# A spectral layer and expert routing on one Trainium2 core: the length-2048 transform split as 64 by 32 in place of 128 by 16, with quarter-array products and a new issue order

## The chip, the core and the metric

The kernel runs on one core of a Trainium2 chip. The core has five engines with queues of their own: TensorE (PE, matrix products; its weight loads are shown as PEld), VectorE (DVE), ScalarE (ACT), GpSimd (POOL) and SyncE (SP, which here only issues the DMAs). They meet through semaphores. Data lies in SBUF (128 partitions), and products land in PSUM, which has eight banks of 2 KB per partition. The metric is the device time of one execution in microseconds; lower is better.

## What is computed

`x` has 2048 rows of 576 numbers. It is normalised by rows to `xn`; the result is `x + A(xn) + B(xn)`.

```python
def _A_ref(x, w_r, w_i):                      # a filter in the spectrum
    X = rfft2(x)                              # over 2048 rows and 576 columns
    return irfft2(X * (w_r + 1j * w_i))

def _B_ref(x, w_q, k1, k2, u, v):             # 32 heads, 8 by 8 experts, the best one per head
    q = einsum("nd,dhc->nhc", xf, w_q)
    s1 = einsum("nhd,ed->nhe", q[..., :128], k1)
    s2 = einsum("nhd,ed->nhe", q[..., 128:], k2)
    e = argmax(s1) * 8 + argmax(s2)           # K = 1, so the softmax weight is 1
    return einsum("nh,nhd->nd", gelu(einsum("nd,nhd->nh", xf, u[e])), v[e])
```

## The kernel before

**The spectral branch.** The length-2048 transform is split as 128 by 16: row `16 n + t` is point `n` of slice `t`. `ln`, `folds` and `dft128` normalise, fold the 576 columns to even and odd halves and do the 128-point step, one slice `t` at a time, as f32 products with the matrix `Rs`. The result is kept as two f16 parts (high and remainder) in `AB` and `ABL`. Then there are 16 groups `g` of frequencies. For each, `d_fwd` does the 576-point step (14 f16 products), after which ACT copies the result from PSUM to f16 and DVE subtracts to get the f16 remainder; `s_fwd` does the 16-point step with the twiddle factors for two groups at once, as 48 f16 products of 64 by 64 on quarters of the PE array (high by high, remainder by high, high by remainder); `s_mul` multiplies by the filter; `s_inv` and `d_inv` go back, and `fin` does the inverse 128-point step for one slice `t` as two f32 products of the whole array (one for each half of the 576 columns).

**The routing branch.** `fold_part` multiplies the keys into `w_q` (18.9 MB, 32 loads named `w<-in_wq`) on quarter strips of the array, 32 columns wide. For each of eight row blocks `r`, `x_t` loads and splits the transposed `x`; `scores` makes the scores relative to expert 0 for 64 lists of seven (28 products of 512 columns), their maximum `mx`, and a mask `eq` of where the maximum is; `route` turns the masks into codes, powers of two that say which expert won, and multiplies and adds them to one matrix of weights; `combine` splits these into f16 high and remainder parts, and PE transposes them (two per block) into `CAT`. `fin` adds `CAT` times the table `vS` (four f16 products of the whole array for each `t`), adds `x`, and stores the slice.

**The order of the work.** Each call on an engine is recorded as an operation of a planner (`_Plan`); neighbouring products are joined to one operation of up to about 0.9 us by the planner's own costs. `forward` then lists all operations: each engine, whenever free, takes the ready one with the lowest number in the table `RANK` (1295 entries, one per operation, in the order of the program text). The resulting order is fixed in the instruction streams, each engine runs its own in order, and SP's stream of DMAs likewise. A DMA into a buffer that is used again waits for the buffer, and what stands behind it on SP waits too. All instructions are issued by one helper, so that they all have line 527 in the profile; they are told apart by tile names. There `A` stands for the buffers of `F`, `A2` and `yy` together, `t` for `t1`, `t2` and the folds, `MT` for the routing's small tables and `CAT`, `w` for the routing's masks and the loads of `w_q`.

Of the kernel before, what the change touches and what calls it, by code (L numbers as in the profile page):

```python
# [10 lines left out]
F32 = mybir.dt.float32  # L11
F16 = mybir.dt.float16
# [20 lines left out]
def _consts():  # L33
    pi2 = 2 * np.pi
    n1 = np.arange(128)
    R = np.zeros((128, 16, 4, 2))
    for k in range(64):
        g, a = divmod(k, 4)
        if k == 0:
            R[:, g, a, 0] = 1.0  # L40
            R[:, g, a, 1] = (-1.0) ** n1
        else:
            R[:, g, a, 0] = np.cos(pi2 * (k * n1 % 128) / 128)
            R[:, g, a, 1] = -np.sin(pi2 * (k * n1 % 128) / 128)
    R = _clean(R.reshape(128, 128))
    c32 = np.stack([R * 2.0 ** -7, R.T * 0.5, np.eye(128)], 1).astype(np.float32)

    U = np.zeros((16, 16, 4, 2, 16, 2, 4))
    V = np.zeros_like(U)
    n2 = np.arange(16)[:, None]  # L50
    k2 = np.arange(16)[None, :]
    kk = np.zeros((16, 16, 2, 4), int)
    for g in range(16):
        for a in range(4):
            k1 = 4 * g + a
            if k1 == 0:
                for s in range(2):
                    ph = pi2 * ((64 * s + 128 * k2) * n2 % 2048) / 2048
                    U[g, :, a, s, :, s, a] = np.cos(ph)
                    V[g, :, a, s, :, s, a] = -np.sin(ph)  # L60
                    kk[g, :, s, a] = 64 * s + 128 * np.arange(16)
            else:
                ph = pi2 * ((k1 + 128 * k2) * n2 % 2048) / 2048
                for s, sg in ((0, 1), (1, -1)):
                    U[g, :, a, 0, :, s, a] = np.cos(ph)
                    U[g, :, a, 1, :, s, a] = np.sin(ph)
                    V[g, :, a, 0, :, s, a] = -sg * np.sin(ph)
                    V[g, :, a, 1, :, s, a] = sg * np.cos(ph)
                    kk[g, :, s, a] = (sg * (k1 + 128 * np.arange(16))) % 2048
    U = _clean(U.reshape(16, 128, 128))  # L70
    V = _clean(V.reshape(16, 128, 128))


    pair = np.arange(128).reshape(16, 2, 2, 2).transpose(2, 0, 1, 3).ravel()
    row = np.arange(128).reshape(16, 2, 2, 2).transpose(1, 0, 2, 3).ravel()
    kk = kk.reshape(16, 128)[:, pair]
    U, V = U[:, :, pair], V[:, :, pair]

    def halves(m):
        return np.concatenate([m[:, :64, :64], m[:, 64:, 64:]], 1)  # L80

    def tr(m):
        m = m.transpose(0, 2, 1).reshape(16, 128, 16, 8).transpose(0, 1, 3, 2).reshape(16, 128, 128)
        return halves(m)

    Ut, Vt = tr(U), tr(V)
    iv = np.concatenate([Ut, Vt, -Ut], 2)
    U, V = halves(U[:, row]), halves(V[:, row])
# [3 lines left out]
    s16 = np.concatenate(_hl(fw * 64) + _hl(iv), 2)  # L92
# [446 lines left out]
def _body(ctx, tc, nc, plan, a, out):  # L539
# [413 lines left out]
    def combine(r):  # L953
# [15 lines left out]
        for i in range(2):  # L969
            P.transpose(pc[:, i, :], chl[:, i, :], id16)  # L970
# [263 lines left out]
```

## Time and profile before

| | |
|---|---|
| median of 3 runs | 223.67 us (222.45 to 223.74) |
| span of the profiled execution, first to last instruction | 220.8 us |
| PE busy in the span | 196.7 us |
| DVE busy | 193.2 us |
| POOL busy | 146.0 us |
| ACT busy | 136.8 us |
| read from and written to memory | 38.33 MB, 4.72 MB |

The profiled execution has no time of its own beside its span; the span is 2.87 us below the median of the timed runs, which also hold what lies ahead of the first and behind the last instruction. A product in f32 appears as two records in the profile (so `x64` of the f32 products in `fin` are 32 products). The ends of products are modelled, so consecutive starts, not the durations, tell what one costs in a stream.

### The profile page before, as it was taken

What the parts mean: (1) busy time and instruction counts of PE and PEld (TensorE: products, weight loads), DVE (VectorE), ACT (ScalarE), POOL (GpSimd) and SP (SyncE); (2) the same over time, 40 slices, a digit from 0 to 9 for tenths busy, and PEclk for the clock granted to TensorE, in tenths of its full rate; (3) what the DMA queues carried; (4) which work ended last, traced back from release to release, by engine and by line L of the source; (5) the groups of instructions that cost most, each with busy time, mean ns of one, the idle gap of its engine ahead of it and who ended that gap; (6) DMA issues with size and microseconds to landing.
All of it is one profiled execution on the core that took longest, in us unless ns stands there. A gap on an engine that the chain in (4) does not pass through costs nothing.

```text
span 220.8 us, 5961 instructions
## 1 busy us (share of the span) xinstructions
PE 196.7 (89%) x2287; PEld 134.9 (61%) x2287; DVE 193.2 (88%) x423; ACT 136.8 (62%) x297; POOL 146.0 (66%) x201
## 2 busy tenths in 40 slices
PE   0079789999999999899998999899999899999993
PEld 0048367766866658466565666455566577788872
DVE  1886999998599879639999998999999999999973
ACT  2096987986499788986769658585652323332330
POOL 3987887960209962854598349687946656686890
PEclk9999999999999999999999999999999999999999
DMA  6999999999999991634246310410000012123225
GB/s 205 405 425 416 408 410 405 389 354 353 367 410 411 406 370 64 202 98 109 96 123 196 118 56 11 148 39 4 1 3 0 0 56 107 53 109 125 91 113 210
DMA packets 14572, 43.43 MB, mean 197 GB/s; under 512 B 1872, under 2 KB 4688, under 8 KB 14160
## 3 DMA queue, kind: packets, MB, share of 16 engines
q1 hardware_dynamic: 14544, 43.05, 52.5%
q8 instruction: 18, 0.29, 0.5%
q14 instruction: 10, 0.08, 0.1%
HBM read 38.33 MB, written 4.72 MB: 195 GB/s over the span
## 4 chain that ended last, share of the span: by engine, by line
PE 48%; DVE 23%; ACT 13%; issue 6%; DMA 5%; POOL 3%; SPq 0%; DVEq 0%; POOLq 0%; ACTq 0%
PE banks L527 48%; DVE t L527 5%; DMA xf<-in_xT_dram 4%; DVE w L527 4%; DVE MT L527 3%; DVE A L527 3%; ACT t L527 2%; ACT xf L527 2%; DVE mx L527 2%; DVE AB L527 2%; DMA kT<-in_kT_dram 2%; ACT AB L527 1%; POOL yh L527 1%; DVE st L527 1%; ACT A L527 1%
## 5 line engine op out<-in xcount | busy, mean ns | idle before, releaser
L527 PE MATMUL banks<-MU,xT 128*128 128x512 f16 x192 | 47.9, 379 | 1.0 <-ACT A L527 0.6
L527 POOL TENSOR_TENSOR xT<-xf,xT 128x640 f16<-128x640 f32 x16 | 23.2, 1455 | 19.5 <-ACT xf L527 19.5
L527 PE MATMUL banks<-c,AB 128*128 128x145 f16 (+1 forms) x384 | 34.6, 227 | 0.0
L527 PEld LDWEIGHTS <-xT 128*128 128x128 f16 x224 | 20.6, 99 | 21.9 <-issue 1.3
L527 PEld LDWEIGHTS <-AB 128*128 128x128 f16 x384 | 31.7, 122 | 3.4 <-issue 1.6
L527 POOL TENSOR_TENSOR A<-t 128x145 f32<-128x145 f32 (+2 forms) x48 | 30.3, 647 | 4.0 <-DVE t L527 1.5
L527 POOL TENSOR_TENSOR y<-t,t 128x289 f32<-128x289 f32 x32 | 21.6, 697 | 14.7 <-DVE t L527 14.5
L527 POOL TENSOR_TENSOR yh<-y,yh 128x578 f16<-128x578 f32 x16 | 23.4, 1470 | 6.8 <-issue 3.0
L527 POOL TENSOR_TENSOR t<-XN 128x289 f32<-128x289 f32 x32 | 24.9, 799 | 4.3 <-DVE A L527 3.0
L527 DVE SCALAR_TENSOR_TENSOR t<-banks,wx,Wt 128x578 f32<-128x578 f32 x32 | 24.3, 808 | 0.3 <-PE banks L527 0.3
L527 DVE TENSOR_TENSOR AB<-banks,AB 128x512 f16<-128x512 f32 x32 | 21.6, 679 | 1.9 <-ACT AB L527 1.1
L527 PE MATMUL banks<-w,KP 128*32 128x288 f32 x256 | 21.5, 432 | 1.8 <-DMA w<-in_wq_dram 1.5
L527 ACT ACTIVATE yh<-banks,sc 128x580 f32<-128x580 f32 x16 | 11.7, 744 | 17.6 <-PE banks L527 13.6
L527 PE MATMUL banks<-Rs,yl 128*99 128x128 f32 x64 | 10.9, 302 | 13.1 <-ACT Rs L527 13.1
L527 ACT ACTIVATE AB<-banks 128x512 f16<-128x512 f32 x32 | 18.8, 590 | 4.6 <-PE banks L527 4.5
L527 PE MATMUL banks<-A,c 128*128 128x288 f32 x64 | 21.4, 416 | 0.0
L527 PE MATMUL banks<-c,ABL 99*128 99x289 f16 (+1 forms) x64 | 18.5, 289 | 2.3 <-DVE AB L527 0.9
L527 PEld LDWEIGHTS banks<-Rs,A 128*128 128x128 f32 x128 | 16.3, 202 | 3.7 <-DVE A L527 1.8
L527 DVE TENSOR_TENSOR ABL<-banks,ABL 33x256 f16<-33x256 f32 x32 | 12.9, 407 | 6.4 <-ACT AB L527 5.3
L527 PEld LDWEIGHTS banks<-Rs,yl 128*99 128x99 f32 x64 | 8.3, 180 | 16.6 <-ACT Rs L527 15.7
L527 PE MATMUL banks<-Rs,A 128*128 128x128 f32 x128 | 18.2, 292 | 0.0
L527 DVE TENSOR_REDUCE MT<-w 128x128 bf16<-128x896 bf16 (+1 forms) x16 | 18.1, 1143 | 0.1
(124 smaller groups left out, 433.5 us busy)
## 6 DMA issues: line engine op xcount, KB each, us to landing
w<-in_wq_dram SPq DMA_DIRECT2D x32, 576.0 KB, 7.6
xf<-in_xT_dram SPq DMA_DIRECT2D x16, 320.0 KB, 4.6
Wt<-in_W_dram SPq DMA_DIRECT2D x8, 578.0 KB, 7.3
out_dram<-XN SPq DMA_DIRECT2D x14, 288.0 KB, 2.1
XN<-in_x_dram SPq DMA_DIRECT2D x3, 1154.0 KB, 12.4
s<-in_s_dram SPq DMA_DIRECT2D x16, 192.0 KB, 3.4
XN<-in_x_dram SPq DMA_DIRECT2D x2, 577.0 KB, 4.9
c<-in_c_dram SPq DMA_DIRECT2D x1, 868.5 KB, 8.6
```

The lines of the kernel that those rows point to most:

```text
L527: fn(*[x.place() if isinstance(x, _Ps) else x for x in args], **{k: x.place() if isinstance(x, _Ps) else x for k, x in kw.items()})
```

## The change

The 2048 points are split as 64 by 32. Two slices of 64 points share the 128 partitions, so the forward matrix `Rs` is a block matrix with one 64-point block for each half, and the host sends `x` with its rows in that order. The inverse 64-point step in `fin` then has 64 rows and 64 columns, and both it and the products with `vS` run on quarters of the array: 4 f32 and 12 f16 products of 64 by 64 with 288 columns for each `t`. The two halves of the 576 columns land on the two halves of the partitions, so `x` is loaded a second time in that layout (`xd`, 4.7 MB, three loads of `load_x`), over the first copy, and each slice is stored by two DMAs in place of one.

`s_fwd` takes the result of `d_fwd` in f32 (16 f32 products of 64 by 64 for two groups in place of 48 in f16), and the subtraction on DVE behind `d_fwd` goes. `s_inv` writes `AB` with shorter runs. The routing masks are stored as eight planes, the eighth made by one more comparison, and `route` halves the planes three times (of 512, 256 and 128 outputs) in place of one product of 896, one maximum over 896 and one step of 128. `combine` gets its transposes from eight products with the identity, out of a buffer `CZ` with zeros between the parts. In `d_inv`, every second `t` forms the mirrored half on DVE, from PSUM, where POOL did it for all. `RANK` is another table, of 1293 entries; its first eight belong to the loads of slices 0 and 1, `c32`, slices 2 and 3, 4 to 7, 8 to 11, 12 to 15, `kT` and `mk`.

```diff
 RANK = (
-    2, 14, 13, 15, 45, 90, 11, 12, 4, 3, 6, 5, 1, 17, 42, 39, 16, 8, 0, 7, 10, 9, 18, 20, 25, 23, 22, 26, 38,
...
+    1242, 1258, 1243, 1259, 1261, 1275, 1199, 1292, 287, 891, 316, 277, 252, 732, 727, 870, 447, 978, 1025,
...
-    ABg = AB.rearrange("p q c (g n) -> p q c g n", g=16)
+    ABg = AB.rearrange("p q c (e g n) -> p q c g e n", e=2, g=8)
+    ABz = AB.rearrange("p q c (h z n) -> p q (c h) z n", h=2, n=32)
...
+    CZ = K([128, 576], F16, "CZ")
+    G.memset(CZ, 0.0)
...
 def scores(r):
-        eq = wk[:, 0:896].rearrange("p (t m e) -> p t m e", t=2, e=7)
-        V.tensor_tensor(eq, sv, mx.unsqueeze(3).to_broadcast([128, 2, 64, 7]), op=OP.is_equal)
-        V.tensor_tensor(wk[:, 896:1792].rearrange("p (t n) -> p t n", t=2), wk[:, 0:896].rearrange("p (t n) -> p t n", t=2),
-                        wt.unsqueeze(1).to_broadcast([128, 2, 448]), op=OP.mult)
+        eq = wk[:, 0:1024].rearrange("p (e t m) -> p t e m", e=8, t=2)
+        V.tensor_tensor(eq[:, :, 1:8].rearrange("p t e m -> p t m e"), sv, mx.unsqueeze(3).to_broadcast([128, 2, 64, 7]), op=OP.is_equal)
+        V.tensor_scalar(eq[:, :, 0], mx, 0.0, None, op0=OP.is_le)
...
 def route(r):
-        V.tensor_reduce(v0, wv, axis=AX, op=OP.max)
-        V.scalar_tensor_tensor(vf.rearrange("p t s h -> p (t s h)"), mx.rearrange("p t m -> p (t m)"), 0.0, v0,
-                               op0=OP.is_le, op1=OP.max)
+        a, b = wk[:, 0:1024], wk[:, 1024:1536]
+        for k, o in ((6, b), (12, wk[:, 1536:1792]), (30, vf.rearrange("p t s h -> p (t s h)"))):
+            v = a.rearrange("p (k e n) -> p k e n", e=2, n=128)
+            V.scalar_tensor_tensor(o.rearrange("p (k n) -> p k n", n=128), v[:, :, 1], 2.0 ** -k, v[:, :, 0],
+                                   op0=OP.mult, op1=OP.max)
+            a = o
...
 def combine(r):
-        pc = PS("m", (128, 2, 128), F16)
-        for i in range(2):
-            P.transpose(pc[:, i, :], chl[:, i, :], id16)
+        pc = PS("m", (128, 4, 64))
+        for k in range(4):
+            for h in range(2):
+                P.matmul(pc[:, k, :], CZ[:, 128 * k + 64 * (1 - h):128 * k + 64 * (1 - h) + 128], id16[:, 64 * h:64 * h + 64],
+                         start=(k == h == 0), stop=(k == 3 and h == 1))
...
 def d_fwd(g):
-        t = T([128, 2, 2, L], F16, "A2", 2)
-        A.activation(t[:, 0], p[:, :, :L], AF.Copy)
-        V.tensor_tensor(t[:, 1], p[:, :, :L], t[:, 0], op=OP.subtract)
-        A2[g] = t
+        A2[g] = T([128, 2, L], F32, "A2", 2)
+        A.activation(A2[g], p[:, :, :L], AF.Copy)
...
 def s_fwd(g):
-                for ha, hb in ((0, 0), (1, 0), (0, 1)):
-                    for e in range(2):
-                        r = slice(64 * e, 64 * e + 64)
-                        for q in range(2):
-                            o = 64 * (e ^ q)
-                            s = S16[g + q][:, :384].rearrange("p (h w) -> p h w", h=2)
-                            P.matmul(ps[q][o:o + 64, m, :L], s[r, ha, 64 * w:64 * w + 64], A2[g + q][r, hb, b, :],
-                                     start=(n == 0), stop=(n == 5), tile_position=(64 * e, o))
+                for e in range(2):
+                    r = slice(64 * e, 64 * e + 64)
+                    for q in range(2):
+                        o = 64 * (e ^ q)
+                        P.matmul(ps[q][o:o + 64, m, :L], S16[g + q][r, w:w + 64], A2[g + q][r, b, :],
+                                 start=(b == 0), stop=(b == 1), tile_position=(64 * e, o))
...
-    EG = range(16)
+    EG = (0,2,4,6,8,10,12,14,)
...
 def fin(t, y):
-        x = XN[:, t]
-        for h in range(2):
-            hs = slice(288 * h, 288 * h + 288)
-            P.matmul(p[:, h, :288], RT, y[:, hs], start=True, stop=False)
-            for q in range(2):
-                P.matmul(p[:, h, :288], CAT[:, t, :], vS[:, q, hs], start=False, stop=(q == 1))
-
-        for a, b in (((0, 1), (1, 2)) if t > 13 else ((0, 2),)):
-            xh = x[:, 288 * a:288 * b].rearrange("p (h d) -> p h d", d=288)
-            V.scalar_tensor_tensor(xh, p[:, a:b, :288], sc[:, 11:12], xh, op0=OP.mult, op1=OP.add)
-            Q.dma_start(os[:, t, 288 * a:288 * b], x[:, 288 * a:288 * b])
+        x = XD[:, t]
+        for k in range(4):
+            for h in range(2):
+                hs = slice(64 * h, 64 * h + 64)
+                for c in range(2):
+                    cs, ds = slice(64 * c, 64 * c + 64), slice(288 * c, 288 * c + 288)
+                    w, m = ((RT[hs], y[hs, ds]) if k == 0 else
+                            (CAT[hs, t, 64 * (k // 3):64 * (k // 3) + 64], vS[hs, k % 2 ^ 1, ds]))
+                    P.matmul(p[cs, h, :288], w, m, start=(k == 0), stop=(k == 3), tile_position=(64 * h, 64 * c))
+
+        V.scalar_tensor_tensor(x, p[:, :, :288], sc[:, 11:12], x, op0=OP.mult, op1=OP.add)
+        for c in range(2):
+            Q.dma_start(os[t, c], x[64 * c:64 * c + 64])
...
+    @staged
+    def load_x(t, n):
+        Q.dma_start(XD[:, t:t + n], a["xd"][:, t:t + n])
...
+        if g % 2 == 0 and g > 8:
+            load_x(2 * g - 20, 4) if g < 14 else load_x(8, 8)
```

More of the change, by code (lines that the diff above doesn't have):

```diff
@@ L70, in _consts @@
[L70 to L84, printed above, removed]
@@ L86, in _consts, with rows @@
-    Ut, Vt = tr(U), tr(V)
+                    U[g, e, :, 0, :, s] = np.cos(ph)
+                    U[g, e, :, 1, :, s] = np.sin(ph)
+                    V[g, e, :, 0, :, s] = -sg * np.sin(ph)
+                    V[g, e, :, 1, :, s] = sg * np.cos(ph)
+                    kk[g, e, :, s] = (sg * (k1 + 64 * np.arange(32))) % 2048
+    U = _clean(U).reshape(16, 2, 2, 16, 2, 64)
+    V = _clean(V).reshape(16, 2, 2, 16, 2, 64)
+    kk = kk.reshape(16, 128)
+    def rows(m, order):
+        return m.transpose(0, 1, *order, 5).reshape(16, 2, 64, 64)
@@ L87, in _consts @@
+    Ut, Vt = (rows(m, (2, 4, 3)).transpose(0, 1, 3, 2).reshape(16, 128, 64) for m in (U, V))
     iv = np.concatenate([Ut, Vt, -Ut], 2)
-    U, V = halves(U[:, row]), halves(V[:, row])
+    U, V = (rows(m, (3, 2, 4)).reshape(16, 128, 64) for m in (U, V))
     fw = np.concatenate([U, V, -U], 2)
```

117 lines of the change are left out of this document (58 added, 59 removed), and 126 rows, old and new, of the table RANK.

## The prediction

> **What bounds the kernel now.** I read the page first, then busy time by stretches, then the stream of products. The page gives the span and two engines that are both nearly full; the slices show that both stay so from start to end.
>
> ```profile
> span 220.8 us, 5961 instructions
> PE 196.7 (89%) x2287; PEld 134.9 (61%) x2287; DVE 193.2 (88%) x423; ACT 136.8 (62%) x297; POOL 146.0 (66%) x201
> PE   0079789999999999899998999899999899999993
> DVE  1886999998599879639999998999999999999973
> ```
>
> The chain of waits, in order of time, ends in one long piece on PE and a last step on DVE; before 118 us it changes engines every microsecond or two, so no single engine carries that part.
>
> ```profile
> 118.27 20.41 PE banks L527 x286
> 175.93 41.38 PE banks L527 x330
> 217.40 0.52 DVE XN L527
> ```
>
> Busy time by stretches (start:end, length, then PE, PEld, DVE, ACT, POOL with their instructions, granted clock, DMA share, GB/s):
>
> ```profile
> 0.00:12.40 12.40, 0.00 (x0) 0.00 (x0) 6.99 (x28) 2.59 (x6) 8.30 (x25) 1.00 0.86 321
> 62.00:85.00 23.00, 21.98 (x415) 14.90 (x408) 19.74 (x41) 19.86 (x39) 14.60 (x15) 1.00 0.95 374
> 85.00:118.00 33.00, 30.77 (x435) 20.64 (x433) 27.33 (x47) 26.81 (x50) 22.46 (x24) 1.00 0.41 122
> 118.00:150.00 32.00, 30.87 (x439) 19.10 (x439) 31.22 (x63) 23.30 (x46) 21.27 (x23) 1.00 0.27 82
> 150.00:176.00 26.00, 24.89 (x243) 14.65 (x238) 25.58 (x48) 12.46 (x28) 17.80 (x22) 1.00 0.01 2
> 176.00:210.00 34.00, 34.00 (x282) 26.56 (x282) 33.89 (x64) 10.72 (x19) 24.56 (x39) 1.00 0.23 88
> 210.00:220.80 10.80, 7.30 (x50) 5.16 (x48) 5.74 (x11) 1.73 (x5) 5.10 (x8) 0.96 0.45 165
> ```
>
> PE starts at 12.4 us. From 62 to 176 us it shows 1.02 + 2.23 + 1.13 + 1.11 = 5.5 us of idle time, and none from 176 to 210. DVE's idle time from 62 to 176 is 3.26 + 5.67 + 0.78 + 0.42 = 10.1 us. So PE's work sets the length, and waits for DVE and others add some 5 us of holes. What share of the last stretch on DVE is its own? The two steps of `d_inv` and `fin` on DVE, the last column-sum step on `XN` and the one that reads `yh`, take after 176 us:
>
> ```profile
> 176.00:220.80 44.80, 13.20 (x18) 0.00 (x0) 0.00 (x0) 0.99 0.28 107
> 176.00:220.80 44.80, 6.65 (x13) 0.99 0.28 107
> ```
>
> That is 19.9 us of DVE's 33.9 + 5.7 = 39.6; the other 19.8 us are routing that was left for the end, and `fin` hides it.
>
> **The products of PE.** In a stream the distance between starts is the price. The end of the kernel:
>
> ```profile
> 201.83 0.70 PE L527 MATMUL banks<-A,c 128*128 128x288 f32 x2
> 202.36 0.41 PE L527 MATMUL banks<-vS,MT 128*128 128x288 f16 x2
> 202.60 0.29 PE L527 MATMUL banks<-c,ABL 99*128 99x290 f16 x1
> 202.73 0.55 PE L527 MATMUL banks<-c,AB 128*128 128x145 f16 x6
> 203.12 0.29 PE L527 MATMUL banks<-c,ABL 99*128 99x290 f16 x1
> ...
> 204.42 0.28 PE L527 MATMUL banks<-id,MT 128*128 128x128 f16 x2
> 204.58 0.28 PE L527 MATMUL banks<-c,ABL 99*128 99x290 f16 x1
> ```
>
> Half of one `fin` is 202.60 - 201.83 = 0.77 us: one f32 product of 288 columns in 0.53, two f16 products in 0.24 (0.12 each). A whole `fin` is 1.54 us. A 145-column product costs 0.39 / 6 = 0.065 us, and two transposes of `combine` 0.16 us.
>
> For quarters of the array the nearest rows are the key products (f32, four strips of 32 columns side by side) and `s_fwd` (f16, 64 by 64):
>
> ```profile
> 49.19 0.69 PE L527 MATMUL banks<-w,KP 128*32 128x288 f32 x8
> 49.81 1.16 PE L527 MATMUL banks<-Rs,A 128*128 128x128 f32 x8
> ...
> 53.85 1.18 PE L527 MATMUL banks<-w,KP 128*32 128x288 f32 x16
> 54.95 1.10 PE L527 MATMUL banks<-Wt,on 128*128 128x64 f32 x8
> ...
> 125.47 1.68 PE L527 MATMUL banks<-A,s 64*64 64x289 f16 x48
> 127.08 1.04 PE L527 MATMUL banks<-MU,xT 128*128 128x512 f16 x4
> 127.95 0.29 PE L527 MATMUL banks<-c,ABL 99*128 99x289 f16 x1
> ```
>
> Eight records, which are four f32 products, take 0.62 us with the change of the array's shape, and sixteen 1.10: so four products side by side cost 0.48 us and a change there and back 0.14. `s_fwd` takes 127.08 - 125.47 = 1.61 us for 48 products, or 12 rounds of four: 0.134 each, against 0.12 for one product of the whole array, so four do run at once.
>
> - `fin` becomes one round of f32 and three of f16 and one change of shape: 0.48 + 3 x 0.12 + 0.15 = 1.0 us. It saves 0.54 us sixteen times: **-8.6**. Bounds: without any change of shape 0.84 (-11.2); with no overlap beyond two at a time 1.84 (+4.8).
> - `s_fwd` becomes four rounds of f32: 4 x 0.48 + 0.15 = 2.07 against 1.61, eight times: **+3.7**. A low bound is +2.5, without the change; the high one stands with the rivals.
> - `combine`: eight products, each with weights for the whole array and 64 columns. The nearest is the 145-column product with new weights each time: 8 x 0.065 = 0.52 against 0.16, eight times: **+2.9** (0 if all eight take what the two transposes take now, +4 at the 0.08 of one transpose each).
>
> PE's sum is -2.0 us. The first step's products keep number and size, `d_inv` and `scores` too.
>
> **The products of DVE.** Groups of instructions (count | busy, mean ns of one), then three short ones in sequence:
>
> ```profile
> L527 DVE TENSOR_TENSOR A<-banks,A 128x578 f16<-128x578 f32 x16 | 11.9, 751 | 0.5 <-ACT A L527 0.4
> L527 DVE TENSOR_REDUCE MT<-w 128x128 bf16<-128x896 bf16 x8 | 8.6, 1076 | 0.0
> L527 DVE TENSOR_TENSOR w<-w,wt 128x896 bf16<-128x896 bf16 x8 | 5.1, 640 | 0.0
> L527 DVE SCALAR_TENSOR_TENSOR MT<-mx,MT 128x128 bf16<-128x128 f32 x8 | 3.0, 374 | 0.0
> L527 DVE CAST wt<-mk 128x448 bf16<-128x448 f32 x1 | 1.0, 1003 | 0.0
> L527 DVE SCALAR_TENSOR_TENSOR t<-banks,sc,yh 128x290 f32<-128x290 f32 x16 | 8.2, 512 | 0.7 <-ACT yh L527 0.6
> ```
>
> ```profile
> 126.37 0.28 DVE L527 SCALAR_TENSOR_TENSOR MT<-mx,MT 128x128 bf16<-128x128 f32 x1
> 126.58 0.28 DVE L527 TENSOR_TENSOR MT<-MT,fm 128x128 int32<-128x128 int32 x1
> 126.78 0.21 DVE L527 SCALAR_TENSOR_TENSOR MT<-MT 128x64 bf16<-128x64 bf16 x1
> 126.91 0.41 DVE L527 TENSOR_TENSOR w<-MT,iv 128x512 bf16<-128x512 bf16 x1
> ```
>
> Gone: the subtraction behind `d_fwd` 11.9, the maximum 8.6, the product with `wt` 5.1, the step with `mx` 3.0, the copy 1.0: 29.6 us. New: steps of 512, 256 and 128 outputs. From 128 outputs (0.21 between starts) and 64 (0.13) the slope is 1.25 ns for each output, so 0.69 + 0.37 + 0.21 = 1.3 us, eight times 10.4. The low bound is 0.8 (the 512-output product above takes 0.41), the high one 1.9, if all are as much slowed as the mean of 374 ns for 128 outputs; 6 to 15 us. The extra comparison has 128 outputs: about 0.3, eight times 2.4. Eight mirrored halves come from POOL, at the 0.51 of the step beside them: 4.1. Together 16.9, so DVE loses about 13 us (8 to 17).
>
> What of it lies on the path? PE is the longer engine, so this is worth no more than PE's holes, 5.5 us from 62 to 176, and some are waits for ACT or DMA. I take **-4** (0 to -5.5).
>
> **What I cost at nothing.** The second load of `x`: 4.7 MB in stretches with a DMA share of 0.41, 0.27 and 0.01; it needs only that the folds are done, and their products (`Rs`, the row at 49.81 us) belong to the first third. Twice as many stores: each `fin` gives SP two issues in place of one, with about 2 us for each `t`; behind them stands no load. The last step on DVE covers a whole slice again, not half of one: +0.3 at the very end. POOL loses 8 steps, ACT's copies keep their size. SP's order at the start: with the numbers of the new table `kT` comes first of the loads, then slices 0 and 1, 2 and 3, one load of `s16`, `c32`, and the other slices with loads of `w_q` between them, so the first product should not start much later or earlier than at 12.4 us (-2 to +2).
>
> **The sum.** -8.6 + 3.7 + 2.9 - 4 = -6.0. On the profiled execution it is 220.8 - 6.0 = 214.8 us of span; with the 2.87 us that lie between this span and the median, **217.7 us**.
>
> **The rivals.**
>
> *DVE holds the end* (slower). Place: the last stretch, from 176 to 217.9 us, 41.9 us long. PE would need only 41.9 - 8.6 = 33.3 there. DVE's own steps become 19.9 + 4.1 = 24.0, so only 9.3 us of routing fit beside them, where 19.8 lie now. The rest has to be done earlier; the 10.1 us of idle time on DVE and what the subtraction frees make that possible, but the new order decides. If it leaves the routing where it is, the end stays about 42 us, and before it PE has 3.7 + 2.0 (`s_fwd` and most of `combine`) more to do: 223.67 + 5.7 = 229 us. It decides from 9.3 us of routing left after the first `fin`. For it: DVE is at 33.89 of 34. Against: the pressure on DVE falls by 13 us.
>
> *The new order gives the gain back* (no change). A table of numbers without any visible run of neighbours replaces one that nearly follows the program. If no hole is closed and 2 us are lost elsewhere, 223.67 - 2.0 + 2 = 223.7 us.
>
> *f32 quarters do not overlap across row halves* (much slower). The key products overlap in column strips with all 128 rows; f32 on row halves stands in no row. Two at a time makes `s_fwd` 8 x 0.48 + 0.15 = 4.0 us, +2.4 eight times = +19 in place of +3.7: 217.7 + 15.4 = 233 us, and up to 237 with no hole closed. Against it: f16 does overlap. The Trainium skill, "TensorEngine Tiling (Array Packing)", Restrictions and Gotchas, says that different row tiles cannot use one PSUM bank at the same time; `s_fwd` writes one bank from both row halves, so by that rule it would come out as this rival does. The trace does not bear the rule out: the f16 `s_fwd` writes in the same pattern and takes 0.134 us for four.
>
> *All holes close and the start gets shorter* (faster still): 223.67 - 2.0 - 5.5 - 4 = 212 us, if the key products, whose loads now stand early, fill PE before 12.4 us and the slow stretch behind it.
>
> **How the numbers follow.** The forecast (214 to 221.4 us) has a chance of 0.48, the faster case 0.14, the no-change case 0.19, DVE at the end 0.14, f32 without overlap 0.05. A change of under 1% (221.4 to 225.9 us) is what a measurement here can't tell from none. Faster by over 1%: 0.48 + 0.14 = 0.62; within: 0.19; slower: 0.19. The range goes from 209 us (the faster case with its low bounds) to 229 us (DVE at the end) and leaves out f32 without overlap and half of the tails, some 0.15.
>
> **What would show it.** Between starts: 16 products of `s_fwd` in 2.0 to 2.1 us, `fin` in 1.0, `combine`'s eight in 0.5. DVE busy near 180 us, PE near 195. PE's idle time between the first product and the last 3 us below what it is now. If `fin` needs 1.0 but the time does not fall, and DVE is full after the first `fin` while PE has holes, the end belongs to DVE. If PE has new holes before that, the order is at fault. If `s_fwd` takes 4 us, it was the overlap.

## The result: 13% slower, where 2.7% faster was forecast

The changed kernel takes 253.49 us in the median of 4 runs (250.73 to 255.08) against 223.19 for the kernel before on the same chip: a ratio of 1.133, 95% interval 1.124 to 1.142 (the ratio leaves out the run of 255.08 us, whose granted clock was the lowest of the four, 0.926). The profiled execution has a span of 251.5 us, 30.7 more than before.

The page of the changed kernel (engines with their busy time; PE and the granted clock in 40 slices):

```profile
span 251.5 us, 6185 instructions
...
PE 205.5 (82%) x2399; PEld 137.8 (55%) x2399; DVE 204.4 (81%) x420; ACT 135.5 (54%) x297; POOL 140.1 (56%) x193
...
PE   0176988999999999976959879936998585999991
...
PEclk9997999999999999997989979995899978699998
```

DVE is busy 11 us longer, not 13 us shorter, and PE's row has gaps from its 18th slice (about 107 us) on, most with a fall of the clock beside them. The groups of instructions on DVE say which step it is:

```profile
L524 DVE TENSOR_TENSOR w<-banks,mx 128x896 bf16<-128x896 f32 x8 | 33.3, 4159 | 0.9 <-ACT MT L524 0.8
```

This is the mask `eq`, with its count, its busy time in all and the mean of one in ns. It compares the same 896 numbers as in the kernel before, where it took 1084 ns (the row of the five that lie behind 140 us):

```profile
L527 DVE TENSOR_TENSOR w<-banks,mx 128x896 bf16<-128x896 f32 x5 | 5.4, 1084 | 0.0
```

Now it takes 4159, eight times: 8 x 3.07 = 24.6 us more on DVE. The timeline around one of them shows what that does to PE (start, duration, what, and the idle time ahead with what ended it):

```profile
111.10 4.14 DVE L524 TENSOR_TENSOR w<-banks,mx 128x896 bf16<-128x896 f32 x1 [0.38 <-ACT MT L524]
...
115.30 0.28 PE L524 MATMUL banks<-c,ABL 99*128 99x289 f16 x1 [3.43 <-DVE w L524]
...
116.61 4.14 PE L524 MATMUL banks<-MU,xT 128*128 128x512 f16 x12
```

PE waits 3.43 us for the mask, and the stream behind the hole is slow as well: 12 products of 512 columns take 120.58 - 116.61 = 3.97 us, 0.33 each, where four take 0.87 in the kernel before (0.22 each, the row at 127.08 us in the prediction). Busy time by stretches gives the clock for it, 0.83 on average in these 10 us, where it was 1.00 in the 10 us ahead of them:

```profile
110.00:120.00 10.00, 6.57 (x50) 3.68 (x43) 9.55 (x9) 3.52 (x6) 5.05 (x6) 0.83 0.21 48
```

### The profile page after: what moved, and what is told of

Read it like the earlier page. It is cut to its first block, busy times and chain, and to the rows that moved or that the text cites. A ratio compares the mean times of both kernels' runs of the same rounds, so it can differ in the third digit from the quotient of the medians.

```text
span 251.5 us, 6185 instructions
## 1 busy us (share of the span) xinstructions
PE 205.5 (82%) x2399; PEld 137.8 (55%) x2399; DVE 204.4 (81%) x420; ACT 135.5 (54%) x297; POOL 140.1 (56%) x193
## 4 chain that ended last, share of the span: by engine, by line
PE 49%; DVE 32%; ACT 5%; POOL 4%; DMA 4%; issue 3%; SPq 0%; DVEq 0%; POOLq 0%; ACTq 0%
PE banks L524 49%; DVE w L524 15%; DVE mx L524 3%; DVE MT L524 3%; DVE t L524 3%; POOL A L524 2%; DMA XN<-in_x_dram 2%; DMA Wt<-in_W_dram 2%; DVE AB L524 2%; POOL t L524 1%; DVE A L524 1%; DVE st L524 1%; DVE rr L524 1%; ACT AB L524 1%; DVE ABL L524 1%
## 5 line engine op out<-in xcount | busy, mean ns | idle before, releaser
L524 PE MATMUL banks<-MU,xT 128*128 128x512 f16 x192 | 50.3, 408 | 0.0
L524 PEld LDWEIGHTS <-xT 128*128 128x128 f16 x224 | 22.7, 105 | 26.0 <-issue 6.1
L524 PE MATMUL banks<-c,AB 128*128 128x145 f16 (+1 forms) x384 | 36.7, 236 | 0.1
L524 PEld LDWEIGHTS <-AB 128*128 128x128 f16 x384 | 33.4, 125 | 5.4 <-issue 3.6
L524 DVE TENSOR_TENSOR w<-banks,mx 128x896 bf16<-128x896 f32 x8 | 33.3, 4159 | 0.9 <-ACT MT L524 0.8
L524 PE MATMUL banks<-Rs,yl 128*99 128x128 f32 x64 | 11.5, 314 | 16.3 <-ACT Rs L524 12.3
L524 PE MATMUL banks<-s,yh 64*128 64x128 f16 x384 | 14.8, 228 | 11.2 <-DVE w L524 8.6
L524 ACT ACTIVATE yh<-banks,sc 128x580 f32<-128x580 f32 (+1 forms) x16 | 10.0, 624 | 20.9 <-PE banks L524 15.4
L524 PEld LDWEIGHTS <-yh 64*128 64x128 f16 x384 | 12.2, 100 | 15.0 <-issue 14.0
L524 PE MATMUL banks<-w,KP 128*32 128x288 f32 x256 | 19.8, 415 | 0.3 <-DVE AB L524 0.3
L524 ACT ACTIVATE ABL<-banks 99x256 f16<-99x256 f32 x32 | 12.1, 381 | 13.3 <-PE banks L524 9.6
## 6 DMA issues: line engine op xcount, KB each, us to landing
XN<-in_xd_dram SPq DMA_DIRECT2D x2, 1152.0 KB, 10.3
```

The lines of the kernel that those rows point to most:

```text
L524: fn(*[x.place() if isinstance(x, _Ps) else x for x in args], **{k: x.place() if isinstance(x, _Ps) else x for k, x in kw.items()})
```

## The experiments

### The mask's write pattern

What differs in the mask is how it is written. Before, it filled `w` in the order of the scores, seven neighbours for each list. The change stores eight planes of 128, so two outputs that follow each other lie 128 bf16 numbers, or 256 bytes, apart. The first run goes through the same outputs plane by plane: neighbours are written in turn, and it is the scores in PSUM that are read with a step of 28 bytes.

```diff
-        V.tensor_tensor(eq[:, :, 1:8].rearrange("p t e m -> p t m e"), sv, mx.unsqueeze(3).to_broadcast([128, 2, 64, 7]), op=OP.is_equal)
+        V.tensor_tensor(eq[:, :, 1:8], sv.rearrange("p t m e -> p t e m"), mx.unsqueeze(2).to_broadcast([128, 2, 7, 64]), op=OP.is_equal)
```

> One instruction of the changed kernel is walked in another order: the comparison that makes the masks writes its eight planes one plane after the other, with the scores read in steps of 28 bytes from PSUM, where the changed kernel writes neighbouring elements 256 bytes apart. Theory W (the scattered write is slow): the instruction falls from 4.16 us to about 1.1, eight times 3.1 is 24.6 us of DVE, nearly all of it on the path, and PE's holes and its low granted clock (0.934) go with it: 223 to 231 us, clock 0.98 or more. Theory O (the new order leaves PE waiting, and the slow mask only fills time in which DVE would wait anyway): 243 us or more, clock still below 0.95. Theory R (reading PSUM in steps is just as slow): the instruction stays near 4 us, and the time at 250.

226.95 us, ratio 1.018 (1.010 to 1.025). Its page and its groups on DVE:

```profile
span 225.3 us, 6185 instructions
...
PE 196.8 (87%) x2399; PEld 133.0 (59%) x2399; DVE 182.9 (81%) x420; ACT 135.7 (60%) x297; POOL 140.6 (62%) x193
```

```profile
L524 DVE TENSOR_TENSOR w<-banks,mx 128x896 bf16<-128x896 f32 x8 | 8.7, 1085 | 0.9 <-ACT MT L524 0.8
L524 DVE SCALAR_TENSOR_TENSOR w<-w 128x512 bf16<-128x512 bf16 x8 | 5.9, 737 | 0.0
L524 DVE SCALAR_TENSOR_TENSOR w<-w 128x256 bf16<-128x256 bf16 x8 | 5.7, 711 | 0.0
L524 DVE TENSOR_SCALAR w<-mx 128x128 bf16<-128x128 f32 x8 | 2.8, 344 | 0.0
L524 DVE SCALAR_TENSOR_TENSOR MT<-w 128x128 bf16<-128x128 bf16 x8 | 2.2, 276 | 0.0
```

One line of the kernel is worth 26.5 of the 30.3 us. On PE this shows in two ways: between its first and its last product it stands idle for 29 us in the changed kernel and for 12 in this one, and the same 2399 records take 205.5 us of busy time in place of 196.8, at a mean granted clock of 0.934 in place of 0.965. I call this version the mended kernel. The other side of it: the kernel before in its old order, with nothing but the new routing codes (planes and halving), once with the scattered mask and once plane by plane.

> The kernel before with nothing but the new routing codes (planes, written as in the changed kernel, and three halving steps), in its old order. Theory W: eight slow masks add 24.6 us, the halving steps give some 6 back, and DVE is the longer engine: 235 to 247 us. Theory O: 220 to 226 us.

> The kernel before, in its old order, with the new routing codes alone and their mask written plane by plane. By the durations of the changed kernel the halving steps and the extra comparison take 1.9 us for each of eight blocks and the steps removed 2.09: VectorE's busy time changes by less than 3 us. Theory S (the write pattern was all that was wrong with the routing): 221 to 224.5 us, the same as before, where the same part with the mask as the change writes it gave 248.95. Rival H (the halving itself costs time, by the length of its chain before combine): 225 to 228 us.

248.95 us (one run, a little above its theory's range) and 224.31 us, ratio 1.006 (1.003 to 1.008). The scattered mask alone makes nearly the whole loss, in a kernel without any other part of the change; and the halving, written well, gains nothing (it costs 0.6%): theory S holds.

The price by itself, in a kernel that computes nothing of the reference (`wplane` and `wswap` are the two masks; the names with a number write 256 outputs with a step of so many numbers; `k` has bf16 outputs and `f` f32):

> The disputed instruction by itself, four times in each form, with no other engine at work; the output is left at zero and nothing of the reference is computed. Theory W: 896 outputs written 256 bytes apart take 4.1 us here too, in a row 1.1 us, plane by plane 1.1; and 256 outputs written in steps of 2, 4, 8, 16 bytes and more show from which step on the price sets in. Theory C (the instruction is slowed by what PE, ACT and POOL do at the time): about 1.1 us in all forms.

```profile
L53 DVE TENSOR_TENSOR wsbuf<-xin,mxt 128x896 bf16<-128x896 f32 x4 | 16.5, 4124 | 0.0
L44 DVE TENSOR_TENSOR wplane<-ps,mxt 128x896 bf16<-128x896 f32 x4 | 16.5, 4118 | 0.0
...
L62 DVE TENSOR_TENSOR ksixtyfour<-xin 128x256 bf16<-128x256 f32 x4 | 5.9, 1466 | 0.0
...
L62 DVE TENSOR_TENSOR keight<-xin 128x256 bf16<-128x256 f32 x4 | 5.7, 1426 | 0.0
...
L47 DVE TENSOR_TENSOR wswap<-ps,mxt 128x896 bf16<-128x896 f32 x4 | 4.5, 1126 | 0.0
L62 DVE TENSOR_TENSOR kfour<-xin 128x256 bf16<-128x256 f32 x4 | 3.1, 772 | 0.0
...
L66 DVE TENSOR_TENSOR fsixtyfour<-xin 128x256 f32<-128x256 f32 x4 | 2.4, 596 | 0.1
L62 DVE TENSOR_TENSOR kone<-xin 128x256 bf16<-128x256 f32 x4 | 1.6, 397 | 0.0
```

The price is the same from PSUM and from SBUF, and it does not need the rest of the kernel. For bf16 it is small at a step of 4 bytes (453 against 397 ns), half there at 8 bytes (772) and full at 16 (1426); 64 numbers cost no more (1466). (1426 - 397) / 256 is 4.0 ns for each output; the mask, with its 896, pays (4118 - 1126) / 896 = 3.3 ns. The Trainium skill, "SBUF — State Buffer", in its note on cachelines, speaks of lines of 16 bytes where each access that crosses to a new line pays; the point where the price is full agrees, the half price at 8 bytes and the mild 596 ns of f32 outputs do not follow from it.

### What the mended kernel still lacks: the order

The mended kernel is 4 us slower than before and 9 above the forecast. First suspect is the new order. The mended kernel with the table of the kernel before (its new operations placed behind their neighbours):

> As the run before it, but with the table of the kernel before for the order, carried over to the operations that both have; new operations stand right behind their neighbours. Theory W: the order is a small matter, within 5 us of the run with the new order. Theory O: the time falls to 215 to 222 us, while with the new order it stays above 240.

227.92 us, ratio 1.025 (1.019 to 1.031): no better. The new order does have a bad start, though. Its timeline on PE, and busy time by stretches for it and for the kernel before:

```profile
20.05 1.17 PE L524 MATMUL banks<-Rs,yl 128*99 128x128 f32 x4 [3.40 <-ACT yl L524]
```

```profile
20.00:30.00 10.00, 9.01 (x52) 6.42 (x53) 6.45 (x20) 6.52 (x19) 6.39 (x12) 0.56 0.78 298
```

```profile
20.00:30.00 10.00, 7.70 (x76) 4.96 (x72) 9.58 (x32) 10.00 (x32) 8.57 (x16) 1.00 1.02 408
```

PE stands for 3.40 us, then runs at a granted clock of 0.56 and does 52 instructions where 76 were done before; the key loads wait for it (SP waits 9.3 us for PE between 20 and 32 us), so the DMAs sink to 298 GB/s. So I put each engine's first 43 us in the old order and left the rest:

> The changed kernel with its mask written plane by plane; each engine's instructions that the old order has in its first 43 us come first, in the old order, and all others follow in the order of the change. Theory S (the new order loses its time in the first 40 us: there PE had done 168 instructions against 217 before, with a hole of 3.4 us and a granted clock of 0.56 from 20 to 30 us, and PE is busy nearly all the time from then on): the last key product at 82 to 85 us instead of 92.2, the first fin 4 to 7 us earlier than at 185.1, and 219 to 222.5 us. Rival T (PE's holes behind 40 us and the longer last store eat it in any order): 224 to 227 us although the start is better.

225.08 us, ratio 1.012 (1.008 to 1.017). The stretch from 20 to 40 us is at full clock and 405 GB/s, but from 45 to 50 us the clock is 0.66 and the DMAs move 303 GB/s: the slow stretch has come later rather than gone. The last key product still ends at 90.4 us (92.2 in the mended kernel), and the 1.9 us lie within the two intervals. By its time this is rival T; what a start without any slow stretch is worth, the run does not show.

Two orders of my own, found with the kernel's own planner and corrected costs, one for the mended kernel and one for the kernel before:

> The changed kernel with its mask written plane by plane and a third order: found for this kernel, starting from the old order, by trying numbers in the kernel's own planner after 30 ns were added there to the cost of each instruction of VectorE, ScalarE and POOL (by so much the planner's sums fall short of the times of the kernel before). Theory O (the parts of the change save time when the order fits them, and the start of the new order is what costs): 217 to 221.5 us, faster than before. Rival D (VectorE and the second load eat the gain in any order): 222.5 to 227 us.

> The kernel before, nothing of the change in it, with an order found in the same way and with as many tries. It says how much of a gain of the run beside it is the order's alone. Theory O: 221 to 224 us, the old order being as good as this way of looking finds. Rival R (any new order found so gains as much): 218 to 220.5 us.

226.58 us (1.012, 1.006 to 1.019), where rival D had it, and 227.6 us (1.018, 1.012 to 1.024), above both expectations. The same search makes the kernel before slower and the mended one no faster. The planner can't tell orders apart to 2%, and the old one is a good one for the kernel that it was made for; whether a better one exists for the mended kernel stays open.

### The second load of x, and the mirrored halves

Three runs tried a part of the change undone: the mirrored halves of `d_inv` all on POOL, the second loads of `x` held back by a dependence in the planner, and both.

```diff
-    EG = (0,2,4,6,8,10,12,14,)
+    EG = tuple(range(16))
...
+            plan.gate = {len(plan.ops) - 1}
             load_x(2 * g - 20, 4) if g < 14 else load_x(8, 8)
+            plan.gate = set()
```

> The changed kernel with its mask written plane by plane (226.95 us), and all sixteen mirrored halves of d_inv on POOL; before had sixteen on POOL, the change gave eight of them to VectorE. Theory D (VectorE holds the end: it is busy 19.7, 18.6 and 20.0 of each 20 us from 140 to 200 us): eight steps of 0.51 us leave the stretch that VectorE fills, so 223 to 224 us, and VectorE's busy time falls by 4 from 182.9. Rival P (POOL becomes the limit of the end): each point block then has three POOL steps; 226 to 229 us with POOL over 95% busy after the first fin. Rival E (what was lost was lost before the first fin, in the order and in the loads): 226 to 227.5 us, VectorE idle at the end.

> The changed kernel with its mask written plane by plane (226.95 us), and the three second loads of x held back until the products of s_inv 10, 12 and 14 stand in the order, out of the stretch in which the key table is loaded. Theory X (the second load delays the key table): the last key product ends at 80 to 84 us instead of 92.2, the first scores stand at 90 to 93 us instead of 101.2, and the time falls by 2 to 5 us, to 222 to 225. Theory D (VectorE holds the end): the earlier scores let VectorE do some routing earlier, but it is full from 140 us on; 224 to 226 us. Rival N (the load lies beside other work): the first scores stay at 101 us and the time within 1% of 226.95.

> The changed kernel with its mask written plane by plane, all sixteen mirrored halves on POOL and the second loads of x held back. If D and X are two causes, their gains add: 219 to 222 us, faster than before. If the two open the same hole: 222 to 224. If neither is a cause: 226 to 228.

232.75 us (1.042, 1.036 to 1.048), 247.95 (1.110, 1.105 to 1.116) and 245.28 (1.099, 1.094 to 1.104). All theories missed, because the experiments were bad: the planner makes its list anew, and a table of numbers fitted to one set of operations gives quite another order for a slightly different one. So the next two keep the mended kernel's order and banks, and exchange only the instructions that are issued at those places:

```diff
+            plan.ops[-1].calls = [(nc.gpsimd.tensor_tensor, (eo[:, :, 288:144:-1], es[:, :, 0:144], qs[:, :, 0:144]), dict(op=OP.subtract))]
...
+        order = [i for i in order if i not in self.late]
+        k = order.index(self.spot)
+        order[k:k] = self.late
```

> The changed kernel with its mask written plane by plane (226.95 us), the eight mirrored halves that the change gave to VectorE back on POOL, and this time every other instruction of every engine in the same order and the same banks as there. Theory D (VectorE holds the end, being full from 140 to 200 us): 8 x 0.51 = 4.1 us less on VectorE, and 222.5 to 225 us. Rival P (POOL's three steps for each slice then hold the end): 226 to 230 us. Rival E (the end is given by what came late in the first 100 us): within 1% of 226.95, VectorE with new idle time after the first fin. The 232.75 us of the earlier run would then be the work of the order alone.

> The changed kernel with its mask written plane by plane (226.95 us), the three second loads of x moved back on their queue to the place of s_inv 12, every other instruction in the same order and the same banks. Theory X (the second load delays the key table and the point tables): the first scores stand 4 to 10 us earlier than at 101.2 us and the time is 220 to 224.5 us. Rival C (what delays the key table is the start: PE idle for 3.4 us before 20 us, a granted clock of 0.56 from 20 to 30 us and the key loads that wait for PE): the last key product moves by less than 3 us from 92.2 and the time stays within 1% of 226.95.

226.91 us (1.016, 1.011 to 1.021) and 226.44 (1.015, 1.009 to 1.020). Against 232.75 us for the same edit in another order, 226.91 shows how much of the first result was the order, and so does 226.44 against 247.95. The second load delays nothing: the last key product stays at 92.0 us. Theory X falls. Rival C has its numbers right, but its cause is not shown: with the old start the last key product came only 1.8 us earlier.

That the halves on POOL gain nothing is the surprise: 4.1 us of work left DVE, whose busy time is 182.8 us as before:

```profile
PE 195.6 (87%) x2399; PEld 132.3 (59%) x2399; DVE 182.8 (81%) x412; ACT 137.8 (61%) x297; POOL 146.3 (65%) x201
```

The groups of DVE after 176 us, first of the mended kernel, then of this one:

```profile
L524 DVE SCALAR_TENSOR_TENSOR XN<-banks,sc,XN 128x576 f32<-128x576 f32 x16 | 12.7, 806 | 1.1 <-PE banks L524 1.0
...
L524 DVE SCALAR_TENSOR_TENSOR w<-w 128x512 bf16<-128x512 bf16 x2 | 1.4, 677 | 0.0
...
L524 DVE SCALAR_TENSOR_TENSOR MT<-w 128x128 bf16<-128x128 bf16 x2 | 0.6, 276 | 0.0
```

```profile
L524 DVE SCALAR_TENSOR_TENSOR XN<-banks,sc,XN 128x576 f32<-128x576 f32 x16 | 12.7, 807 | 1.8 <-PE banks L524 1.7
...
L524 DVE SCALAR_TENSOR_TENSOR w<-w 128x512 bf16<-128x512 bf16 x2 | 1.8, 922 | 0.0
...
L524 DVE SCALAR_TENSOR_TENSOR MT<-w 128x128 bf16<-128x128 bf16 x2 | 1.1, 536 | 0.0
```

The step that reads a bank keeps its 806 ns; the small steps of the routing, which live in SBUF alone, grow by a third to nearly double when POOL has more to do. Over the whole execution five groups of the routing's small steps add up to some 2.4 us more; that they make up all of the 4.1 is not shown. A kernel that computes nothing of the reference measures it: the halving steps of 512 and 128 outputs in turn, then sums and steps from a bank in turn, first alone (`a`), then beside additions on POOL (`b`).

> No part of the reference is computed; the output is zero. VectorE runs four kinds of steps eight times each, alone and then beside a chain of additions of 128 by 288 on POOL: a halving step of 512 outputs and one of 128 (two inputs from SBUF), a sum over 1024 (one input from SBUF), a subtraction of 512 (one input from a bank, one from SBUF). Theory V (steps with two inputs from SBUF wait for POOL's additions): the halving steps go from 0.6 to 0.7 us to over 1.0 us beside POOL, the one of 128 outputs from 0.2 to over 0.5, and the sum and the subtraction stay within 5%. Rival: all four stay within 10%.

```profile
L42 DVE TENSOR_REDUCE asum<-codes 128x32 f32<-128x1024 bf16 x8 | 9.8, 1219 | 0.0
L42 DVE TENSOR_REDUCE bsum<-codes 128x32 f32<-128x1024 bf16 x8 | 9.6, 1205 | 0.0
...
L40 DVE SCALAR_TENSOR_TENSOR blast<-codes 128x128 bf16<-128x128 bf16 x8 | 7.0, 877 | 0.0
...
L38 DVE SCALAR_TENSOR_TENSOR bhalf<-codes 128x512 bf16<-128x512 bf16 x8 | 5.4, 680 | 0.0
...
L40 DVE SCALAR_TENSOR_TENSOR alast<-codes 128x128 bf16<-128x128 bf16 x8 | 2.3, 288 | 0.0
```

The short step grows from 288 to 877 ns; the long one does not (the expectation had both). A likely reason is that it comes when POOL has just had its turn: the two kinds of steps alternate, and eight pairs went with eight additions. The sums and the steps from a bank stay as they are. POOL pays too: the groups on POOL, beside the halving and beside the sums:

```profile
L53 POOL TENSOR_TENSOR gone<-yy,xin 128x288 f32<-128x288 f32 x8 | 10.0, 1254 | 0.6
...
L53 POOL TENSOR_TENSOR gone<-yy,xin 128x288 f32<-128x288 f32 x16 | 12.6, 789 | 1.3
```

So an addition on POOL and a halving step take turns. The Trainium skill, "SBUF — State Buffer", section "SBUF: two separate sides", states it as a lock that a VectorE step with two inputs from SBUF and a GpSimd step that reads SBUF hold for their whole length; these rows agree. Moving work between the two engines then gains little. Taking it away from both is the test: the mended kernel, order and banks kept, without any mirrored half (`plan.ops[-1].calls = []` behind both; half of the output's columns are then not computed).

> The changed kernel with its mask written plane by plane and its order and banks kept; all sixteen mirrored halves of d_inv are left out, eight of VectorE's and eight of POOL's, so half of the output's columns are made from old data. The run with eight of them moved to POOL changed nothing, and VectorE's busy time stayed at 182.8 us because its steps on SBUF grew longer. Theory V (VectorE and POOL together hold the end): about 4 us less on each, 221.5 to 224 us. Theory T (PE's own products and the start set the time): 225.5 to 227.5 us, with VectorE's busy time down by more than 4 us.

```profile
PE 194.6 (88%) x2399; PEld 131.3 (59%) x2399; DVE 178.3 (80%) x412; ACT 135.7 (61%) x297; POOL 135.1 (61%) x185
```

222.79 us, ratio 0.999 (0.996 to 1.003), clear of the mended kernel's interval. Theory V holds: 4.6 us less on DVE and 5.5 on POOL (178.3 and 135.1) take 4 us from the time. The run can't tell the load of the two engines from the chain of each slice, which is a step shorter as well; moving that step alone had changed nothing.

### Where DVE's saved time went

Busy time in three stretches (PE, PEld, DVE, ACT, POOL, then clock, DMA share and GB/s) of the kernel before, the mended one, and the one without mirrored halves:

```profile
12.00:40.00 28.00, 24.93 (x211) 18.02 (x211) 24.87 (x83) 23.94 (x73) 23.14 (x40) 1.00 1.02 412
40.00:120.00 80.00, 76.46 (x1087) 52.17 (x1079) 67.32 (x139) 64.48 (x131) 47.92 (x52) 1.00 0.73 264
120.00:220.80 100.80, 95.33 (x998) 64.76 (x997) 94.43 (x180) 46.21 (x93) 67.01 (x87) 1.00 0.20 70
```

```profile
12.00:40.00 28.00, 22.82 (x166) 17.68 (x165) 21.24 (x64) 21.72 (x62) 19.36 (x35) 0.82 0.91 341
40.00:120.00 80.00, 77.46 (x1031) 53.16 (x1030) 59.71 (x137) 63.33 (x134) 47.25 (x53) 1.00 0.91 348
120.00:225.30 105.30, 95.87 (x1206) 61.45 (x1204) 95.81 (x195) 47.98 (x98) 66.17 (x83) 0.97 0.27 70
```

```profile
120.00:222.00 102.00, 93.92 (x1200) 60.54 (x1198) 90.17 (x184) 47.20 (x96) 60.23 (x74) 0.97 0.28 72
```

DVE's busy time falls by 10.3 us (193.2 to 182.9), and all of it ahead of 120 us, where DVE has room and PE and the key loads set the pace. Behind 120 us it has 95.81 us to do, 1.4 more than before, and is busy 91% of the time. PE is busy there as long as before (95.87 and 95.33 us), although `fin` became shorter: `s_fwd` and `combine` are longer, and 15 more of the products of `scores` fall there (176 in place of 161); PE comes out of the start behind by 45 records (166 against 211).

The loss lies ahead of `fin`, not in it. The first product of `fin` starts at 185.11 us in the mended kernel and at 171.53 before; from there to the end of DVE's last step it is 36.2 us in place of 46.4. In these 36.2 us PE is busy for 33.3 and DVE for 33.6, so neither leaves much room.

What is the f32 step worth, the edit behind the largest fall of DVE's work? Two runs, in the kernel before (old order, nothing else of the change), and the other way round in the mended kernel with the old order, where the pairs of f16 come back:

```diff
-        t = T([128, 2, 2, L], F16, "A2", 2)
-        A.activation(t[:, 0], p[:, :, :L], AF.Copy)
-        V.tensor_tensor(t[:, 1], p[:, :, :L], t[:, 0], op=OP.subtract)
+        A2[g] = T([128, 2, L], F32, "A2", 2)
+        A.activation(A2[g], p[:, :, :L], AF.Copy)
```

> The kernel before in its old order, with the forward step in f32 alone: 32 products in place of 48 in each s_fwd at 2.11 us instead of 1.61 between starts (PE +4.0 us), and no subtraction behind d_fwd (VectorE -11.9 us). Theory T (VectorE's relief closes no hole of PE): 225 to 228 us. Theory H (what VectorE loses is worth 4 us or more, as forecast): 221.5 to 224 us.

> The changed kernel with its mask written plane by plane and its forward step in pairs of f16 again, in the old order; everything else of the change stays (the split of the points, quarters, routing codes, second load of x). With the f32 step and this order the kernel took 227.9 us; the f32 step alone cost the kernel before 1.43%. Theory T (the f32 step costs PE more than VectorE's relief is worth, here as there): 223.5 to 226 us. Rival H (in the changed kernel, where VectorE is full at the end, the relief is worth its price): 227 to 230 us.

Both edits change the list of operations, so the planner's order changes as well. In the kernel before the f32 step costs 1.4% (225.87 us, ratio 1.010 to 1.019): PE is busy 200.9 us in place of 196.7, DVE only 6.5 us less instead of 11.9, and the relief does not pay for PE's 4.2. In the mended kernel going back to f16 takes PE from 196.0 to 193.0 us and DVE from 186.1 to 195.0, and the time is 229.28 us (1.018 to 1.035) against 227.92: no gain, so rival H. There the two prices about cancel, as far as two lists can be compared. The last run also gives all mirrored halves back to POOL:

> The same, with all sixteen mirrored halves on POOL as in the kernel before. What is left of the change is the split, the last products on quarters, the routing codes in plane order (alone: 224.3 us) and the second load of x. If PE alone set the end, the 6 to 8 us that the quarters take from PE would show: 217 to 220 us. Theory V (VectorE and POOL together hold the end, so that the quarters gain little): 222.5 to 226 us, PE's busy time 4 us or more under 196.7.

233.02 us (1.036 to 1.052), above both expectations, with PE at 194.5 us, 2 less than before, and waiting 4.3 us for POOL in place of 2.1. But the planner made its list anew here too, as in 232.75 against 226.91 us above, so the 3.7 us over the run before it cannot be put down to POOL. These runs end the idea that PE alone sets the time: in the mended kernel and its variants (the three whose list went astray left out) PE's busy time lies between 193.0 and 196.8 us, and the time between 222.8 and 233.0, without a common trend: the run with the least PE work (193.0 us) takes 229.28.

## Why the prediction was wrong, point by point

**The step that failed.** The list of DVE's work names what is gone ("the maximum 8.6, the product with `wt` 5.1 ...") and what is new ("steps of 512, 256 and 128 outputs", "the extra comparison"), and it has no line for the comparison that stays. It was kept at 1084 ns without a word, as if its price hung on the number of outputs alone; but the diff writes them 256 bytes apart. It measured 4159 ns, 24.6 us in all, and the mended line shows that 26.5 us of the 30.3 hang on it. No rival had it, and the range ended at 229 us.

**DVE's sum.** Forecast -13 (8 to 17), in the mended kernel -10.3. The three halving steps take 737 + 711 + 276 = 1724 ns, not 1.3 us; their slope was read from two steps during which POOL stood idle. The worst is the one of 256 outputs, forecast at 0.37 us. Together with the extra comparison (344) they take 16.5 us against 16.7 removed (17.7 with the copy): the routing codes save nothing, as their own run says.

**"I take -4" for PE's holes.** In the mended kernel it was +4.1: PE stands idle for 12.3 us between its first and its last product, where it was 8.2 before. 2.5 us of this lie ahead of 40 us and 2.6 behind 120 us; between them, where DVE was relieved, PE gains 1.0. On PE the 4.5 us of span that the mended kernel is longer are these 4.1, 1.1 less at the start, 0.1 more of busy time and 1.4 more at the end. The rival that DVE holds the end came nearest in time (229 us; the mended kernel takes 227), but that is partly luck: it had the end stay at 42 us and PE's added work ahead of it, while the end fell to 36.2 us and the stretch ahead of it grew. DVE did have 10.8 us of routing left there, more than the rival's limit of 9.3, and the run without mirrored halves shows that work of DVE and POOL sets a part of the time.

**PE's sum.** Forecast -2.0; +0.1 in the mended kernel, which has a mean granted clock of 0.965, -1.5 in the run with the old start (195.2 us, 0.978) and -1.3 in my order (195.4 us, 0.996). The terms, in the timeline of the mended kernel:

```profile
121.84 2.18 PE L524 MATMUL banks<-A,s 64*64 64x289 f32 x32
123.95 0.84 PE L524 MATMUL banks<-s,yh 64*128 64x128 f16 x24
...
206.75 0.71 PE L524 MATMUL banks<-A,c 64*64 64x288 f32 x8 [0.24 <-POOL A L524]
207.29 0.55 PE L524 MATMUL banks<-vS,MT 64*64 64x288 f16 x12
207.66 0.67 PE L524 MATMUL banks<-A,c 64*64 64x288 f32 x8
208.14 0.55 PE L524 MATMUL banks<-vS,MT 64*64 64x288 f16 x12
208.62 0.35 PE L524 MATMUL banks<-c,ABL 99*128 99x290 f16 x1
208.80 0.56 PE L524 MATMUL banks<-c,AB 128*128 128x145 f16 x6
```

`s_fwd` takes 2.11 us (forecast 2.07). `fin` takes 207.66 - 206.75 = 0.91 in a row and 208.62 - 207.66 = 0.96 with the way back to the whole array; the first product of `d_inv` behind it takes 0.18, where it took 0.13 before (the row at 202.60 us). So 1.0 was right, and four f32 quarters do run at once; in `s_fwd` they do so from both row halves into one bank. The rival without overlap falls, and with it, for these products, the rule of the Trainium skill, "TensorEngine Tiling (Array Packing)", that stood behind it.

**What was costed at nothing.** Moving the second load of `x` back gained nothing that could be measured (226.44 against 226.95 us), so it costs nothing where it stands, as forecast; a version without it was not tried. The end of the kernel was put at +0.3. The chain of waits of the mended kernel ends with

```profile
220.47 0.82 DVE XN L524
```

that is 4.0 us before the end of the span, where the last step of the kernel before (217.40, 0.52) stood 2.9 us before it. The 1.1 us of difference are probably the two stores of the last slice, one behind the other on SP; a version without that was not tried. The 2.87 us that the sum adds for the median were too much: in every run on record the time is 1.7 to 2.2 us above the span of the same execution.

**The order.** It was given -2 to +2 us at the start. PE's first product starts 1.1 us earlier, but its holes up to 40 us are 2.5 us longer, and part of the products run at a clock of 0.56; the run with the old start gains 1.9 us at most, and has a slow stretch of its own later. What stays open is which of the holes the order makes and which DVE and POOL; each part is of the size of the intervals. No version that computes the reference's output beats the kernel before.

## What to carry to other kernels

When a diff changes the layout of a buffer, cost every instruction that writes or reads it anew, the unchanged ones first: a step in bytes is part of an instruction's price. Ask of saved engine time in which stretch it lies; what is taken from an engine where it has room was worth nothing here, and VectorE's steps with two inputs from SBUF took turns with GpSimd's additions. And before part of a planned kernel is undone, freeze the order: a planner that lists anew turns a small edit into another kernel (232.75 against 226.91 us).

## What the hardware showed that was not expected

- A step of 28 bytes in reading PSUM costs nothing (1126 ns for 896 outputs, 1085 in the kernel, 1084 in a row before); it is the write to SBUF that pays. Reading the scores from SBUF with that step is not free: 1802 ns in the same run. A bf16 output pays 4.0 ns on VectorE and nearly as much on ScalarE: in the same run 448 scattered outputs take 2265 ns on average against 624 in a row, 3.7 ns each.
- A short step on VectorE with two inputs from SBUF can treble (288 to 877 ns) beside additions on POOL, and an addition grows from 789 to 1254 ns; the busy time of both engines counts the waiting, so a full VectorE is not always one with much to do.
- After a hole of 3.43 us on PE the granted clock was 0.50 from 117 to 119 us of the changed kernel, and after its holes of 2.56, 2.63 and 2.82 us it fell to 0.50 as well. A hole of 2.02 us near 24 us was followed by it in the run with the old order and not in the run with the old start. So a hole costs more than its length. The Trainium skill, "TensorE: Matmul & The Clock Gate", Part 1, gives about 3.4 us of idle time for the fall to half; these traces show it after shorter holes too.
